# Two blocks of hedgehog linear attention and a ReGLU MLP on one core: the attention's inputs, its query side and the MLP's norm are computed in another way, and the plan is made anew

## The chip, the core and the metric

The kernel runs on one core of one Trainium2 chip. The metric is the device time of one execution in microseconds (us). The core's engines are named as in the profile: PE is TensorE's matmul, PEld its weight load, DVE is VectorE, ACT is ScalarE, POOL is GpSimd, and SP is SyncE, whose queue (SPq) issues nearly all DMAs here.

## What is computed

The input `x` has 2048 tokens of 512 bf16 values. Two layers follow each other, each an attention A and an MLP B, both on a layer-normed input and both added to `x`. The same weights serve both layers.

```python
def _A_ref(x, wqkv, w_phi, wo):          # 32 heads of 16
    q, k, v = split(x @ wqkv)
    pq, pk = q @ w_phi, k @ w_phi        # per head, 16x16
    phi_q = concat(softmax(pq), softmax(-pq))
    phi_k = concat(softmax(pk), softmax(-pk))
    kv, z = phi_k^T v, sum_s phi_k       # over all 2048 tokens
    num, den = phi_q kv, phi_q z + 1e-6
    return (num / den) @ wo

def _B_ref(x, W_gate, W_up, W_down):     # 512 -> 1376 -> 512
    return (relu(x @ W_gate) * (x @ W_up)) @ W_down

x = x + _A_ref(_layernorm(x)); x = x + _B_ref(_layernorm(x))   # twice
```

The sums `kv` and `z` run over all tokens. So no query can be answered, and no MLP of that layer can begin, before the keys of all 16 token tiles are summed.

## The kernel before

**Tiles.** The tokens lie in 16 tiles of 128 (`t`), in four chunks of four (`c`). `x` stays in SBUF as `X` and is updated in place. `w_phi` is folded into the key and query weights once, at the start (`fold`, L755 on: turns of the weight by PE, L767, or by DMA, L762, and products with a block-diagonal `Wblk`, L775).

**Attention, keys** (class `Keys`). Each tile is normed on DVE (batch-norm statistics L810 and L811, scale and centre L825; the root on ACT, L818 and L820), and turned to feature-major `xnTA` by PE or by DMA (`turn`, L784 on). PE multiplies it with the folded key weight (L849) and with the value weight (L855). ACT takes Exp of plus and minus the keys (`ek`, L852). DVE sums over each head (L860), ACT makes the reciprocal by Ln and Exp (L867, L870), and DVE or POOL multiply it in, half a tile at a time (`phi`, L879). PE adds the tile to the sums in PSUM with eight 65-column products (L896). After the 16th tile DVE builds the operand `R` (eight pairs, L918 and L924).

**Attention, queries.** The query projection is feature-major: one product gives 128 features for a chunk of 512 tokens (L937), and ACT takes both Exps (L941). In `attend`, PE multiplies a token tile's 128 columns of `Eq` with `R` (eight products of 144 columns, L955): 16 values, the sum of the Exps, and the normalizer for each head. ACT or DVE carry them out of PSUM in six copies (L752, L753). DVE forms the two weights (L971 to L977), multiplies (L980) and adds plus and minus (L985). The result is turned (L787, or L797 on PE), multiplied with `wo` (L992), and added to `X` (L997 for the first two tiles, which also takes the row sum; L1001 for the others).

**MLP** (`mlp`). It goes over groups of 1, 2 or 4 tiles (`BLOCKS`). Each tile gets batch-norm statistics again (L810, L811), is centred (L1018 or L1022) and turned. PE computes gate and up, feature-major, with 128 columns for each tile of the group (L1068), and the last 96 features token-major (L1044). ACT takes the Relu (L1072), ACT or DVE copy `up` out (L752, L753), DVE multiplies (L1076), PE multiplies with `W_down` (L1101), and DVE scales by the reciprocal of the variance and adds to `X` (L1108). For the first layer, the keys of a tile for the second layer begin as soon as its `X` is done.

**What sets the order.** Every operation is recorded as an `Op` with an engine, a cost, a due number and its dependences. `plan` (L82) then walks an event-driven list: it takes the operation that can go first, and the numbers in `DUE` break ties. Its result is the order in which each engine's instructions stand; the chip's engines run them in that order and wait for semaphores. The string `PLACE` chooses the engine of each operation that has two (evacuations and `phi`). PSUM has two banks for the sums and for L955 (`q`), and six for all else (`b`). Until the first L896, gaps that the plan sees on PE are filled with products of zeros (`idle`, L746), so that the clock stays up.

## Time and profile before

| what | value |
|---|---|
| median of 3 runs | 383.91 us (383.69 to 384.04) |
| the profiled execution | span 382.0 us from its first to its last instruction |
| what lies around the span, by the median | 1.9 us |
| granted TensorE clock | 1.00 |
| busy: PE, DVE, ACT, POOL | 371.5, 311.1, 215.0, 41.9 us |
| first L955 (all keys of layer 0 are summed) | 54.4 us |
| first L1068 (first gate product) | 63.86 us |
| first L955 and first L1068 of layer 1 | 237.47 us, 247.38 us |
| the last group of matmuls ends | 378.58 us |

The profile's slices are 9.55 us each. A matmul's duration in the profile is from its start to its result (379 ns for 512 columns), and successive ones overlap: L849 takes 0.86 us for four, so 216 ns each. For PE the spacing counts, not the duration. DVE's and ACT's durations overlap a little too: eight Exps of L941 stand in 4.30 us, 538 ns each, where the duration of one is 629 ns.

### The profile page before, as it was taken

The numbers are of one execution on the slowest core, as the hardware profiler recorded it, in microseconds if no ns is written. First come the engines' busy times: TensorE is split into PE (matmuls) and PEld (weight loads), VectorE is DVE, ScalarE is ACT, GpSimd is POOL, SyncE is SP. The second block draws the span as 40 slices with busy tenths as digits, with TensorE's granted clock in tenths as the row PEclk, the third lists the DMA queues.
The fourth block names the chain that finished last, engine by engine and source line by source line (L and its number), as shares of the span: only waits on it lengthen the run. The fifth ranks groups of instructions, "written<-read, shape, count | busy, mean of one in ns | idle before, by whom it ended". The sixth has DMA issues, their size and how long they took to land.

```text
span 382.0 us, 7622 instructions
## 1 busy us (share of the span) xinstructions
PE 371.5 (97%) x2787; PEld 224.4 (59%) x2832; DVE 311.1 (81%) x798; ACT 215.0 (56%) x554; POOL 41.9 (11%) x44
## 2 busy tenths in 40 slices
PE   7999998999989999999999999999999999999996
PEld 4545456967545445554656654696855544467575
DVE  7999999999999989983694677999998976763334
ACT  6999989636445316772455679984526412243040
POOL 0276710000200000230020124000000000000000
PEclk9999999999999999999999999999999999999999
DMA  8497720222221321211200100013322221020110
GB/s 232 122 205 219 188 89 2 52 58 62 57 56 41 44 54 40 45 23 27 45 6 15 22 8 1 2 36 70 77 44 70 57 56 56 14 62 16 41 50 29
DMA packets 60869, 22.83 MB, mean 60 GB/s; under 512 B 52672, under 2 KB 59808, under 8 KB 60832
## 3 DMA queue, kind: packets, MB, share of 16 engines
q1 hardware_dynamic: 60416, 21.95, 24.9%
q8 instruction: 22, 0.36, 0.4%
q10 hardware_dynamic: 416, 0.39, 0.4%
q14 instruction: 15, 0.12, 0.1%
HBM read 7.91 MB, written 2.10 MB: 26 GB/s over the span
## 4 chain that ended last, share of the span: by engine, by line
PE 77%; DVE 17%; DMA 2%; issue 2%; ACT 1%; DVEq 0%
PE b L1068 31%; PE b L1101 17%; PE b L855 5%; PE b L849 5%; PE b L992 5%; PE b L937 5%; PE q L955 3%; PE b L1044 2%; PE q L896 2%; DMA xnTA<-xn 2%; DVE pr L980 1%; DVE bstA L810 1%; DVE bstB L810 1%; DVE sk L860 1%; DVE N L753 1%
## 5 line engine op out<-in xcount | busy, mean ns | idle before, releaser
L1068 PE MATMUL b<-xnTB,wgu 128*128 128x128 bf16 (+2 forms) x1191 | 152.3, 279 | 0.5
L1068 PEld LDWEIGHTS <-wgu 128*128 128x128 bf16 x1200 | 97.7, 98 | 42.5
L1072 ACT ACTIVATE gu<-b 128x512 bf16<-128x512 f32 (+1 forms) x83 | 48.0, 584 | 63.7 <-PE b L1068 61.3
L1101 PE MATMUL b<-wd,hT 128*128 128x512 bf16 (+3 forms) x349 | 82.3, 372 | 0.7
L879 POOL TENSOR_TENSOR phiK<-ek,sk 128x512 bf16<-128x512 bf16 x38 | 41.2, 1102 | 192.3 <-ACT sk L870 164.1
L1101 PEld LDWEIGHTS <-hT 128*128 128x128 bf16 (+1 forms) x363 | 34.7, 98 | 33.9 <-DVE hT L1076 0.2
L1076 DVE TENSOR_TENSOR hT<-gu 128x512 bf16<-128x512 bf16 (+1 forms) x83 | 34.0, 414 | 15.4 <-ACT gu L752 14.2
L1108 DVE SCALAR_TENSOR_TENSOR X<-b,rsB,X 128x512 bf16<-128x512 f32 (+1 forms) x33 | 23.7, 729 | 23.8 <-PE b L1101 23.8
L752 ACT CAST gu<-b 128x512 bf16<-128x512 f32 (+1 forms) x50 | 28.4, 570 | 24.0 <-PE b L1068 20.4
L860 DVE TENSOR_REDUCE sk<-ek 128x64 f32<-128x1024 bf16 x32 | 38.6, 1210 | 2.7 <-ACT ek L852 2.3
L852 ACT ACTIVATE ek<-b 128x512 bf16<-128x512 f32 x64 | 36.0, 616 | 8.3 <-PE b L849 8.1
L941 ACT ACTIVATE Eq<-b 128x512 bf16<-128x512 f32 x64 | 37.3, 629 | 3.3 <-PE b L937 3.1
L752 ACT CAST N<-q 128x384 bf16<-128x384 f32 (+1 forms) x59 | 26.1, 464 | 12.4 <-PE q L955 6.7
L855 PE MATMUL b<-wv,xnTA 128*128 128x512 bf16 x123 | 31.9, 379 | 0.3
L937 PE MATMUL b<-xnTA,Wq 128*128 128x512 bf16 x125 | 31.9, 379 | 0.2
L849 PE MATMUL b<-Wk,xnTA 128*128 128x512 bf16 x123 | 31.6, 379 | 0.4 <-DVE xnTA L753 0.2
L992 PE MATMUL b<-wo,oT 128*128 128x512 bf16 x120 | 31.3, 379 | 0.4
L753 DVE CAST gu<-b 128x512 bf16<-128x512 f32 (+1 forms) x33 | 21.8, 665 | 11.1 <-PE b L1068 11.1
L955 PE MATMUL q<-R,Eq 128*128 128x144 bf16 x256 | 27.5, 226 | 1.8 <-DVE N L753 1.3
L955 PEld LDWEIGHTS <-Eq 128*128 128x128 bf16 x256 | 20.3, 98 | 13.1 <-issue 2.6
L980 DVE TENSOR_TENSOR pr<-N,w 128x1024 bf16<-128x1024 bf16 x32 | 21.8, 683 | 0.7
L810 DVE BATCH_NORM_STATS2 bstA<-X 128x6 f32<-128x512 bf16 x32 | 21.3, 682 | 1.2 <-DMA X<-in_A_x_dram 1.0
(75 smaller groups left out, 388.9 us busy)
## 6 DMA issues: line engine op xcount, KB each, us to landing
out_dram<-X SPq DMA_DIRECT2D x15, 128.0 KB, 1.7
X<-in_A_x_dram SPq DMA_DIRECT2D x6, 256.0 KB, 3.3
wgu<-in_B_W_gate_dram SPq DMA_DIRECT2D x4, 344.0 KB, 3.4
wgu<-in_B_W_up_dram SPq DMA_DIRECT2D x4, 344.0 KB, 3.5
wd<-in_B_W_down_dram SPq DMA_DIRECT2D x5, 256.0 KB, 3.5
wv<-in_A_wqkv_dram SPq DMA_DIRECT2D x2, 256.0 KB, 4.7
wo<-in_A_wo_dram SPq DMA_DIRECT2D x4, 128.0 KB, 3.1
oT<-o SPq DMA_TRANSPOSE x28, 2.3
```

The source lines that it names most:

```text
L752: both = {"ACT": ("ACT", act(cols), lambda: nc.scalar.copy(out=out_(), in_=in_()), False), "DVE": ("DVE", dve(cols), lambda: nc.vector.ten ...
L849: k = op("PE", mm(4, 512), due, lambda: [nc.tensor.matmul(kp.t[:], lhsT=xnTA[c][:, b, cols], rhs=Wk2[:, b, :], start=(b == 0), stop=(b == ...
L855: v = op("PE", mm(4, 512), due_v, lambda: [nc.tensor.matmul(vp.t[:], lhsT=xnTA[c][:, b, cols], rhs=wv[:, b, :], start=(b == 0), stop=(b == ...
L860: a = op("DVE", SUM16, due, lambda: nc.vector.tensor_reduce(out=sk.t[:, row, :], in_=ek.t[:].rearrange("p g s (h f) -> p (g s h) f", f=DH) ...
L879: e.tensor_tensor(out=ph.t[:].rearrange("p g s (h f) -> p (g s h) f", f=DH)[:, lo:lo + n], in0=ek.t[:].rearrange("p g s (h f) -> p (g s h) ...
L937: q = op("PE", mm(4, 512), due(c, b), lambda b=b, qp=qp: [nc.tensor.matmul(qp.t[:], lhsT=Wq2[:, m, b * P:(b + 1) * P], rhs=xnTA[c][:, m, : ...
L941: done.append(op("ACT", act(512), due(c, b), lambda b=b, s=s, qp=qp: nc.scalar.activation(out=Eq[c][:, b, s, :], in_=qp.t[:], func=AF.Exp, ...
L955: pe.append(op("PE", mm(len(groups), GE), due, lambda ps=ps, groups=groups: [nc.tensor.matmul(ps.t[:, n * GE:(n + 1) * GE], lhsT=Eq[c][:, ...
L992: a = op("PE", mm(4, 512), due + 3, lambda: [nc.tensor.matmul(yp.t[:], lhsT=oT.t[:, b, :], rhs=wo[:, b, :], start=(b == 0), stop=(b == NB ...
L1068: nc.tensor.matmul(ps.t[:, q * W:(q + 1) * W], lhsT=wgu[:, s, b, g * P:(g + 1) * P], rhs=xT.t[:, b, 0:W], start=(b == 0), stop=(b == NB - 1))
L1072: nc.scalar.activation(out=gu.t[:, 0, 0:cols], in_=gp.t[:, 0:cols], func=AF.Relu)
L1101: nc.tensor.matmul(yp.t[:, 0:c1 - c0], lhsT=h.t[:m, f * W + i * P:f * W + (i + 1) * P], rhs=wd[:m, f, c0:c1], start=(f == 0), stop=(f == N ...
```

## The change

1. **No normed copy of `x` for the attention.** Keys, queries and values are projected from raw `x`. Its turned copy `xT` comes by DMA straight from the input (layer 0, nine transposes) or from `X` (layer 1). The mean is taken out of the folded weights: `fold` computes each weight row's mean (32 one-column products, a copy, and a bias on the evacuations). The root scales the Exps (`scale=rs` and `-rs`, POOL makes the negative) and the evacuation of the values. What the mean contributes to the values is carried as a 66th column of the sums and taken off when `R` is built. The query weight is now loaded and turned by PE; it was turned by DMA.
2. **Token-major queries.** One query projection gives one token tile. Its Exps are summed on DVE, inverted on ACT, multiplied in place on POOL or DVE, as for the keys, and the 128x1024 result is turned by one DMA (`fq`). So each product with `R` is 68 columns wide and gives the finished numerator and denominator; the denominators are inverted (ACT, or DVE's reciprocal), and one multiply from PSUM writes `o`.
3. **MLP norm from sums.** The residual add takes the row sum for every tile; the sum of squares comes from ACT (`Square`) or DVE. The batch-norm statistics of the MLP go.
4. **`up` without a copy.** Where `PLACE` says DVE (33 of 83), DVE multiplies directly from PSUM; before, it copied and then multiplied.
5. **`phi` in place**, one pool of 22 buffers for keys and queries, seven `fq` buffers, and one PSUM buffer of two banks where two of one bank were.
6. **The plan** has other constants (landings of DMAs, costs, a delay of transposes in flight when PE fetches instructions), new `DUE` and `PLACE`, and each query projection must follow a certain key projection (`QKEY`).

The core of the diff:

```diff
-GV = GQ + 1
-GE = HB * (DH + 2)
+GV = GQ + 2
+GE = HG * (DH + 1)
...
-XPOSE, XPOSE_LOADS = (1245, 3600), (1245, 3600)
+XPOSE, XPOSE_LOADS = (1255, 2440), (1280, 3010)
...
-PHI0 = ["POOL", "POOL", "DVE"] * 5 + ["BOTH"]
-SUM_ON_PE, SPLIT, SUMMED = False, False, 2
+SUM_ON_PE, SPLIT = False, False
+QKEY = ((10, 11, 12, 13, 14, 15), (12, 13, 14, 15))
...
-    p_q, p_b = psum("q", 2), psum("b", 6)
+    p_q, p_b = psum("q", 1, [NG, P]), psum("b", 6, [512])
...
+        mp = Buf(p_b)
+        a = op("PE", (16 * 32, 16 * 32 + 170, 16), due, lambda: [nc.tensor.matmul(
+            mp.t[:, b:b + 1], lhsT=w[:, m, b * P:(b + 1) * P], rhs=less[:, 0:1], start=(m == 0), stop=(m == NB - 1))
+            for b in range(NB) for m in range(NB)], loaded + [c_less], [mp], name="means")
...
             e = [op("ACT", act(512), due, lambda s=s: nc.scalar.activation(
-                out=ek.t[:, :, s, :], in_=kp.t[:].rearrange("p (g e) -> p g e", e=GQ), func=AF.Exp, scale=1.0 - 2.0 * s), ...
+                out=ek.t[:, :, s, :], in_=kp.t[:].rearrange("p (g e) -> p g e", e=GQ), func=AF.Exp,
+                scale=(minus if s else plus)[:, t:t + 1]), [k, root[s]], ...
...
+    def query(l, t, due, ready, behind, key):
+        q = op("PE", mm(4, 512), due, lambda: [nc.tensor.matmul(
+            qp.t[:], lhsT=xT[c][:, b, cols], rhs=Wq2[:, b, :], ...) for b in range(NB)], ...)
+        e = [op("ACT", act(512), ..., func=AF.Exp, scale=(minus if s else plus)[:, t:t + 1]) for s in range(2)]
+        a = op("DVE", SUM16, ..., name="sq", follow=behind)
+        a = op("ACT", RLN[0], ..., name="lnq")
+        a = op("ACT", REXP[0], ..., name="rq")
+        a = halves("phq", ek, lambda: ek.t[:], lambda lo, n: sq.t[:, lo:lo + n], PHI["POOL"], ...)
+        a = op("SP", XWIDE, due, lambda: nc.sync.dma_start_transpose(
+            out=fq.t[:], in_=ek.t[:].rearrange("p g s e -> p (g s e)")), a, [fq], [ek], name="fq", move=1450)
...
+        pe = [op("PE", SUMS, due, lambda: [nc.tensor.matmul(
+            ps.t[:, g, 0:GE], lhsT=fq.t[:, g, :], rhs=R[:, g, :], start=True, stop=True) for g in range(NG)], ...
+        a = op("DVE", dve(512), due, lambda: nc.vector.tensor_tensor(out=o..., in0=ps.t[:, :, 0:GQ]..., in1=rd..., op=Alu.mult)
...
-            a = stats(l, "B", t, due_x(i), [after[t]])
+            seen.append(op("ACT", SQUARE, due_x(i), lambda t=t: nc.scalar.activation(
+                out=wasteA[:], in_=x_of(t), func=AF.Square, accum_out=ssq[:, l, t:t + 1]), [after[t]], name="ssq", ...
...
+            def direct(up=up, gu=gu, cols=cols, f0=f0):
+                nc.vector.tensor_tensor(out=h.t[:, f0 * W:f0 * W + cols], in0=gu.t[:, 0, 0:cols], in1=up.t[:, 0:cols],
+                                        op=Alu.mult)
```

How many instructions stand on each engine, as the two programs are built (DMA issues under SP):

| | before | after |
|---|---|---|
| PE, matmuls | 2832 | 2867 |
| of them the products with `R` | 256 of 144 columns | 256 of 68 columns |
| DVE | 794 | 531 |
| ACT | 555 | 564 |
| POOL half-tile multiplies (`phi`) | 38 | 86 |
| DVE half-tile multiplies (`phi`) | 26 | 42 |
| SP, all; transposes of 128x512 or smaller; of 128x1024 | 149; 101; 0 | 175; 87; 32 and 7 of 256 tokens |

## The prediction

> **What bounds the kernel now.** First the page's head, then the busy time by stretches. I cut at the first product with `R` (L955), the first gate product (L1068) and the first gate product of layer 1.
>
> ```profile
> span 382.0 us, 7622 instructions
> PE 371.5 (97%) x2787; PEld 224.4 (59%) x2832; DVE 311.1 (81%) x798; ACT 215.0 (56%) x554; POOL 41.9 (11%) x44
> ...
> PE 77%; DVE 17%; DMA 2%; issue 2%; ACT 1%; DVEq 0%
> ```
>
> ```profile
> 0.00:54.40 54.40, 51.76 (x378) 26.67 (x386) 50.34 (x105) 48.40 (x132) 23.91 (x28) 1.00 0.72 185
> 54.40:63.86 9.46, 8.03 (x66) 4.82 (x67) 8.54 (x28) 9.29 (x29) 0.00 (x0) 1.00 0.00 0
> 63.86:247.38 183.52, 180.99 (x1317) 108.76 (x1337) 154.96 (x389) 105.78 (x271) 17.95 (x16) 1.00 0.17 34
> 247.38:382.00 134.62, 130.73 (x1032) 84.20 (x1044) 97.30 (x278) 51.49 (x126) 0.00 (x0) 1.00 0.20 48
> ```
>
> The columns are PE, PEld, DVE, ACT, POOL, clock, DMA share, GB/s. From 63.86 us on PE hardly waits: it is the bound. In the first 54.4 us PE, DVE and ACT are all nearly full, so there no engine's gain counts alone.
>
> A matmul's duration overlaps its neighbours', so I take PE's cost from spacing in the timeline:
>
> ```profile
> 50.19 0.67 PE L896 MATMUL q<-vext,phiK 128*128 128x65 bf16 x16
> 50.70 1.02 PE L937 MATMUL b<-xnTA,Wq 128*128 128x512 bf16 x4
> ...
> 65.65 0.48 PE L955 MATMUL q<-R,Eq 128*128 128x144 bf16 x5
> 65.96 0.49 PE L1044 MATMUL b<-wgu,xnTB 128*128 128x192 bf16 x4
> ```
>
> Sixteen 65-column products take 0.51 us to the next start: 32 ns each. Five of 144 columns take 0.31: 62 ns. In the same way 128 columns cost 56 ns, 192 cost 82, 256 cost 109 and 512 cost 216. With the counts in the program, PE's work is 369.4 us. I call **lag** an instruction's start less the work ahead of it. It is 54.4 - 49.3 = 5.1 us at the first L955, 63.9 - 56.5 = 7.4 at the first gate product, 247.4 - 238.1 = 9.3 at that of layer 1, and 378.6 - 369.4 = 9.2 at the end. After the last matmul come 3.4 us (add, store). So span = PE work + lag + 3.4 = 382.0, and the median lies 1.9 us above that span.
>
> **The change, part by part.**
>
> *PE work.* The 256 products with `R` shrink from 144 to 68 columns: at 32 ns, 256 x (62 - 32) = -7.8 us. The means of two weights add 32 one-column products: +1.0. The column sums of the value weight add four of 512 columns, and one filler goes: +0.6. Turns balance (16 of a weight come, 24 of `xn` go, 8 of `X` come). Sum -6.1: 363.3 us. All the rest is lag.
>
> The Trainium skill ("TensorE: Matmul & The Clock Gate", "Back-to-back issue gap") says that in a real stream the spacing also carries the weight load, about 81 ns at 128 columns. The trace disagrees (56 ns; 32 at 65 columns). By the rule narrow products would gain little; that is rival D.
>
> *The front.* Nothing may pass `R`, so the sums ahead of it count, taken in the order of each engine with mean durations. DVE: 55.8 us in 97 instructions before; after, 55.8 in 88. Gone are 16 centrings (L825, 6.4), three half multiplies (2.1) and the fill of `R`; six query sums come (6 x 1.21 = 7.3, the row of L860), and 1.4 for the value sums. ACT up to the last key's reciprocal: 59.5 before, 58.9 after. PE ahead of the first product with `R`: 49.3 before, 53.6 after, because all 16 query projections now stand ahead of it; before, 2.6 us of them stood behind.
>
> So the norm that was removed is replaced, on DVE, by work of the same size. Three things come on top:
> - The first key Exp (10.75 us before) waits for the folded weight, and the fold now needs the means (16 x 32 ns), a copy of 0.17, and all four turned blocks (four evacuations of 0.6 on two engines) where each of its products needed one. I take +1.6; the bounds are 0 (input landing alone decides) and +3.
> - From the first head sum (12.49 us) to `R` (52.52) DVE ran 40.0 us for 43.8 us of durations. After, 46.7 stand there: 42.7 us at that ratio.
> - POOL does 29 half multiplies up to the last key's, where it did 22 in the first stretch. The rows of L879 show what a collision with DVE is:
>
> ```profile
> L879 POOL TENSOR_TENSOR phiK<-ek,sk x38: 1055/1057/1561, 15.7 to 233.2; 128x512 bf16<-128x512 bf16 x38
> ...
> L879 DVE TENSOR_TENSOR phiK<-ek,sk x26: 658/680/1269, 20.5 to 233.2; 128x512 bf16<-128x512 bf16 x26
> ```
>
> The longest are 0.5 to 0.6 us above the median. Eight such DVE multiplies stand ahead of `R`; each may wait between 0 and a POOL multiply (1.06): 0 to 8.5 us. I take two collisions, 1.0, as most of the 26 before ran undisturbed, though POOL was busy for only 23.9 of 54.4 us.
>
> The Trainium skill ("SBUF — State Buffer", "SBUF: two separate sides") calls the port of DVE and GpSimd an exclusive lock: the later of the two blocks for the whole instruction, where DVE reads two SBUF inputs. The trace's tails agree; rival B is what that would cost at worst.
>
> `R` begins at 12.49 + 1.6 + 42.7 + 1.0 = 57.8 us. Its build took 1.9 (52.52 to 54.40); the four new instructions (0.3 + 0.7 + 0.7 + 0.2) take as much. First product: **59.7 us**, work 53.6, lag 6.1.
>
> *From `R` to the first gate product.* Before: 9.46 us, with query projections as filler. After: products 0.45; Ln and Exp of the denominators about 0.55 with gaps (small ACT instructions, 0.22); the multiply 0.7; then turn, `wo`, add, centre and turn as before, 4.97 (58.89 to 63.86 in the timeline); 0.3 for Exps queued ahead on ACT. Sum 7.0 where PE has 3.4 of work, so lag grows by 3.6, against 2.3 before. First gate product: **66.7 us**, lag 9.7.
>
> *The rest.* Between the two `R`s DVE's durations fall from 182 to 158 us, behind the second from 132 to 99 (norm statistics, six copies and four small steps of each tile, direct `up`). That is worth nothing: PE is the bound there. It pays only for cover. ACT falls from 128 to 121 and 81 to 78. Query work that now comes later: ten head sums (12 us on DVE) and 28 half multiplies of layer 0, 21 of them on POOL (22 us), stand behind the last key's. Beside them PE has two one-tile MLPs of 7.2 us (80 x 56 + 4 x 82 + 11 x 216 ns) and the next groups. Two queries are ready to turn before `R`; POOL finishes the next two 3 and 5 us after the last key, and with a landing of 2.3 to 4.6 us they come about when PE reaches them. The 32 wide transposes are not in the trace: issue between one and two narrow ones (1.2 to 2.4 us on SPq), landing between 2.3 (row `oT<-o`) and twice that. SPq waited for data most of the time, and later queries are made many us before use: I take nothing, and up to +3 for late ones. The single PSUM buffer makes the next tile's products wait for this one's multiply, 1.8 us a tile against 8 us of PE work: nothing. At the layer change ACT ran 16.30 of 17 us before (228 to 245); after, 20.8 us of durations stand between the last tile's root and the first turned output, 16.7 with the overlap seen on Exps (538 ns against 629). PE has 18 us of work there. I take +0.5, bounds -0.5 and +3. Lag after the first gate product: 1.8 as before, +0.5.
>
> *Sum.* 363.3 + 9.7 + 1.8 + 0.5 + 3.4 = 378.7 us span; with 1.9, **380.6 us**, 0.9% less than 383.91.
>
> **The rivals.**
> - A, full gain: the start and the lock cost nothing, and lag at the first gate product stays 7.4. 363.3 + 7.4 + 1.8 + 3.4 + 1.9 = 377.8. For: ACT's sum ahead of `R` is smaller, and `x` arrives turned. Against: DVE's equal sum starts later.
> - B, slower: DVE and POOL block each other ahead of `R`. At 0.9 us for each of eight multiplies in place of 1.0 in all, +6.2: 386.8. It decides against the change once the first gate product comes after 70.0 us (lag 13.0, which eats the 6.1). For: POOL nearly without pause. Against: medians 680 and 1057 sit close to the minima.
> - C, late queries: after the first groups PE waits for head sums, multiplies and wide transposes, in all 3 us: 383.6. For: DVE was 97% busy from 60 to 160 us (9.6 to 9.9 of each 10), a small slip spreads. Against: DVE is relieved by 24 us there.
> - D, the narrow products don't get shorter: +7.8, 388.4. Against: the row of L896 above.
>
> **How the numbers follow.** Chances: forecast (378 to 383) 0.58, A 0.17, B 0.13, C 0.10, D 0.02. About 0.2% (383.1 to 384.7) can't be told from no change. Faster is the forecast, A, and a little of C: 0.76; the same 0.09; slower B, D and the rest of C: 0.15. The range, 376.3 to 386.5, takes in A with a little less start lag, C, and the lower part of B.
>
> **What would show it.** Right: the 68-column products spaced at 32 ns; the first at about 59.7 us; the first gate product at about 66.7; PE's lag then growing by some 2 us to the end; DVE with idle time in the MLP stretches. Wrong: a first gate product before 64 (A) or after 70 (B, with long POOL or DVE multiplies before it); PE waiting for `fq` or `oT` behind 70 us (C).

## The result, and the profile after

The changed kernel takes 397.49 us (median of 4 runs, 396.94 to 398.14) where the kernel before takes 383.83 us (4 runs beside it, 383.69 to 384.04): a ratio of 1.0355, with a 95% interval of 1.034 to 1.0369. The change makes the kernel 13.7 us slower. The forecast was 380.6 us, faster, with a range up to 386.5: its sign was wrong, and the time lies outside the range.

The page of the changed kernel, first its head and its chain (time on the path that ended last, by engine):

```profile
span 396.0 us, 7641 instructions
...
PE 370.6 (94%) x2820; PEld 218.7 (55%) x2867; DVE 283.0 (71%) x578; ACT 230.0 (58%) x580; POOL 108.0 (27%) x150
...
PE 53%; ACT 18%; DVE 17%; issue 4%; DMA 4%; POOL 1%; SPq 1%; DVEq 0%; ACTq 0%; POOLq 0%
```

PE's share of the chain fell from 77% to 53%, and ACT's rose from 1% to 18%. An engine that is busy for 58% of the span lies on that chain for some 70 us: the average hides a stage. The stretches, cut at the same three products as before (the first with `R`, the first gate product, the first gate product of layer 1), say which one. Columns: PE, PEld, DVE, ACT, POOL, granted clock, DMA share, GB/s.

```profile
0.00:64.96 64.96, 57.05 (x424) 29.28 (x433) 53.31 (x93) 57.77 (x146) 40.97 (x65) 1.00 0.73 171
64.96:73.71 8.75, 5.13 (x51) 3.26 (x52) 6.79 (x11) 6.47 (x20) 7.96 (x8) 0.80 0.49 92
73.71:261.30 187.59, 180.13 (x1325) 105.55 (x1344) 144.09 (x286) 111.46 (x286) 49.15 (x70) 0.99 0.32 56
261.30:396.00 134.70, 128.32 (x1031) 80.66 (x1043) 78.79 (x191) 54.34 (x130) 9.96 (x10) 0.99 0.35 69
```

The first stretch grew from 54.4 to 65.0 us. ACT's busy time in it grew from 48.4 to 57.8, DVE's only from 50.3 to 53.3. In every 10 us between 10 and 60 us ACT is busy for 9.94 to 10.00; in the kernel before it had been 9.45 to 10.00, between 10 and 50 us. Behind it two further things show: in the second stretch PE works for 5.1 of 8.75 us, at a granted clock of 0.80, and in the third it waits longer than it did before.

In ACT's queue just ahead of `R` the cause can be read. The first column is the start, the second the duration, both in us:

```profile
51.57 0.75 ACT L690 ACTIVATE ek<-b,rsA 128x512 bf16<-128x512 f32 x1
52.14 0.76 ACT L690 ACTIVATE ek<-b,nrs 128x512 bf16<-128x512 f32 x1
52.71 0.77 ACT L764 ACTIVATE ek<-b,rsA 128x512 bf16<-128x512 f32 x1
53.28 0.78 ACT L764 ACTIVATE ek<-b,nrs 128x512 bf16<-128x512 f32 x1
...
64.43 2.05 ACT L764 ACTIVATE ek<-b,nrs 128x512 bf16<-128x512 f32 x3
66.14 0.43 ACT L787 ACTIVATE rd<-q 128x32 f32<-128x32 f32 x1
```

Exps that stand back to back start 570 ns apart. Their inputs are named `b,rsA` and `b,nrs`: besides PSUM they read their scale from a tile in SBUF, the root of the layernorm (L690, L764), which is what the change folded into them. In the kernel before the input is `b` alone, and the starts are 478 ns apart. The last two lines show what that does behind `R`: its first product was issued at 64.96 us, but the Ln of its denominators (L787) began only at 66.14, behind three such Exps of later queries. PE waited for 2.2 us at its next step for it:

```profile
PE b L616 <- DVE o L793: 2.2, 1, 2.2
PE q L783 <- DVE R L745: 1.0, 1, 1.0
PE b L799 <- ACT oT L550: 0.7, 1, 0.7
```

I use the prediction's own measure, the lag (start of an instruction less PE's work ahead of it, by the same spacings), for the kernel before, the forecast, the changed kernel, and three of the experiments below. All in us:

| | before | forecast | changed | e1_const | e13_both_less | e15_all_less |
|---|---|---|---|---|---|---|
| PE work | 369.4 | 363.3 | 363.3 | 363.3 | 363.3 | 363.3 |
| lag, first product with `R` | 5.1 | 6.1 | 11.4 | 4.9 | 4.3 | 3.9 |
| lag, first gate product | 7.4 | 9.7 | 16.7 | 8.9 | 7.4 | 7.2 |
| lag at 110 us of work | 8.6 | | 20.7 | 12.5 | 11.8 | 11.1 |
| lag at 230 us of work | 9.1 | | 21.6 | 13.0 | 12.3 | 11.6 |
| lag at the end of PE | 9.2 | 12.0 | 28.1 | 17.5 | 16.0 | 14.7 |
| behind PE | 3.4 | 3.4 | 4.6 | 4.6 | 3.4 | 3.4 |
| span | 382.0 | 378.7 | 396.0 | 385.4 | 382.7 | 381.4 |

The span missed by 17.3 us: 5.3 ahead of `R`, 1.7 from there to the first gate product, 9.1 behind it, 1.2 behind PE. Two parts of that aren't the change's. The time behind PE lies between 3.4 and 4.6 us in runs that end with the same instructions; the median landing of the two last stores (64 KB) is 2.2 us in the changed kernel and in e1_const, 1.6 in the kernel before and in e13_both_less. And the first key Exp came at 13.67 us in this execution, against 12.14 to 12.58 in three runs below that also keep the changed kernel's Exps (e3_half_turn, e5_late_queries, e9_half_sums_after): more than 1 us of the 5.3 is a late start.

### The profile page after: what moved, and what is told of

The parts are those of the page before. It is cut to its first block, busy times and chain, and to the rows that moved or that the text cites. A ratio compares the mean times of both kernels' runs of the same rounds, so it can differ in the third digit from the quotient of the medians.

```text
span 396.0 us, 7641 instructions
## 1 busy us (share of the span) xinstructions
PE 370.6 (94%) x2820; PEld 218.7 (55%) x2867; DVE 283.0 (71%) x578; ACT 230.0 (58%) x580; POOL 108.0 (27%) x150
## 2 busy tenths in 40 slices
DMA packets 94965, 31.75 MB, mean 80 GB/s; under 512 B 86256, under 2 KB 93904, under 8 KB 94928
## 4 chain that ended last, share of the span: by engine, by line
PE 53%; ACT 18%; DVE 17%; issue 4%; DMA 4%; POOL 1%; SPq 1%; DVEq 0%; ACTq 0%; POOLq 0%
PE b L873 28%; PE b L913 13%; ACT ek L764 6%; ACT ek L690 5%; PE b L799 4%; DVE sq L767 3%; DVE ek L659 2%; DVE sk L703 2%; PE b L849 2%; PE b L687 2%; DVE o L793 2%; PE b L694 2%; DVE X L803 2%; ACT vext L547 2%; DMA oT<-o 2%
## 5 line engine op out<-in xcount | busy, mean ns | idle before, releaser
L913 PE MATMUL b<-wd,hT 128*128 128x512 bf16 (+2 forms) x354 | 83.3, 372 | 0.4
L659 POOL TENSOR_TENSOR ek<-ek,sq 128x512 bf16<-128x512 bf16 x43 | 47.2, 1117 | 52.3 <-ACT sq L772 42.9
L659 POOL TENSOR_TENSOR ek<-ek,sk 128x512 bf16<-128x512 bf16 x43 | 45.6, 1077 | 28.6 <-ACT sk L715 24.2
L703 DVE TENSOR_REDUCE sk<-ek 128x64 f32<-128x1024 bf16 x32 | 38.5, 1212 | 11.6 <-ACT ek L690 11.1
L767 DVE TENSOR_REDUCE sq<-ek 128x64 f32<-128x1024 bf16 x32 | 38.3, 1210 | 3.8 <-ACT ek L764 2.0
L892 ACT CAST gu<-b 128x512 bf16<-128x512 f32 (+1 forms) x50 | 28.1, 562 | 19.3 <-PE b L873 18.8
L890 DVE TENSOR_TENSOR hT<-gu,b 128x512 bf16<-128x512 bf16 (+1 forms) x33 | 22.2, 676 | 15.4 <-PE b L873 15.3
L761 PE MATMUL b<-Wq,xT 128*128 128x512 bf16 x124 | 30.5, 379 | 2.3 <-ACT ek L764 2.0
L687 PE MATMUL b<-Wk,xT 128*128 128x512 bf16 x120 | 31.4, 379 | 1.3 <-ACT ek L690 0.6
L694 PE MATMUL b<-wv,xT 128*128 128x512 bf16 x121 | 31.3, 379 | 1.0 <-DMA xT<-X 0.6
L690 ACT ACTIVATE ek<-b,rsA 128x512 bf16<-128x512 f32 x32 | 22.3, 700 | 3.1 <-PE b L687 3.0
L793 DVE TENSOR_TENSOR o<-q,rd 128x512 bf16<-128x512 f32 x32 | 21.9, 684 | 2.7 <-ACT rd L790 2.6
L764 ACT ACTIVATE ek<-b,rsA 128x512 bf16<-128x512 f32 x32 | 23.5, 766 | 0.0
```

Of the source, the lines that this page charges most:

```text
L659: e.tensor_tensor(out=out().rearrange("p g s (h f) -> p (g s h) f", f=DH)[:, lo:lo + n], in0=ek.t[:].rearrange("p g s (h f) -> p (g s h) f ...
L687: k = op("PE", mm(4, 512), due, lambda: [nc.tensor.matmul(kp.t[:], lhsT=xT[c][:, b, cols], rhs=Wk2[:, b, :], start=(b == 0), stop=(b == NB ...
L690: e = [op("ACT", act(512), due, lambda s=s: nc.scalar.activation(out=ek.t[:, :, s, :], in_=kp.t[:].rearrange("p (g e) -> p g e", e=GQ), fu ...
L694: v = op("PE", mm(4, 512), due_v, lambda: [nc.tensor.matmul(vp.t[:], lhsT=xT[c][:, b, cols], rhs=wv[:, b, :], start=(b == 0), stop=(b == N ...
L703: a = op("DVE", SUM16, due, lambda: nc.vector.tensor_reduce(out=sk.t[:, row, :], in_=ek.t[:].rearrange("p g s (h f) -> p (g s h) f", f=DH) ...
L761: q = op("PE", mm(4, 512), due, lambda: [nc.tensor.matmul(qp.t[:], lhsT=xT[c][:, b, cols], rhs=Wq2[:, b, :], start=(b == 0), stop=(b == NB ...
```

## The experiments

The theories: **O**, the operand: an ACT instruction that reads its scale or bias from SBUF takes 92 ns longer, 149 times, some 75 of them ahead of the first denominators. **T**: the wide transposes of the query features are late or crowd the DMA queue. **P**: the order was made for the wrong prices. **Q**: the three queries that moved ahead of `R` are missing behind it. The kernel before, beside which each group ran, took 383.99 to 384.34 us.

| run | us | ratio to before, 95% interval |
|---|---|---|
| e1_const | 387.22 | 1.0085, 1.006 to 1.011 |
| e2_before_operand | 388.63 | 1.0117, 1.01 to 1.0134 |
| e3_half_turn | 397.91 | 1.0348, 1.031 to 1.0385 |
| e4b_plan_price | 416.22 | 1.0837, 1.0821 to 1.0853 |
| e5_late_queries | 396.49 | 1.0318, 1.0296 to 1.034 |
| e6_late_const | 388.70 | 1.0120, 1.0104 to 1.0136 |
| e7_price_late | 422.61 | 1.1002, 1.0952 to 1.1052 |
| e8_half_sums | 386.25 | 1.0050, 1.0033 to 1.0067 |
| e9_half_sums_after | 397.05 | 1.0332, 1.0315 to 1.035 |
| e10_new_order | 399.61 | 1.0415, 1.0364 to 1.0466 |
| e11_no_inverse | 387.84 | 1.0079, 1.0061 to 1.0097 |
| e12_turn_early | 385.99 | 1.0045, 1.0025 to 1.0065 |
| e13_both_less | 384.96 | 1.0020, 1.0011 to 1.0029 |
| e14_pool_less | 384.46 | 1.0007, 0.9998 to 1.0017 |
| e15_all_less | 383.64 | 0.9986, 0.9972 to 1.0001 |
| e16_both_late | 386.44 | 1.0063, 1.0047 to 1.0078 |

### The operand, taken away and put in

e1_const gives the Exps of the changed kernel the constant scales of the kernel before, and copies the values unscaled:

```diff
-                scale=(minus if s else plus)[:, t:t + 1]), [k, root[s]], [ek] if s == 0 else [],
+                scale=1.0 - 2.0 * s), [k, root[s]], [ek] if s == 0 else [],
...
-                     [v, root[0]] + ones, [vx], [vp], "vext", times=lambda: plus[:, t:t + 1])
+                     [v, root[0]] + ones, [vx], [vp], "vext")
...
-            scale=(minus if s else plus)[:, t:t + 1]), [q, root[s]], (), [qp, ek], name="Eq") for s in range(2)]
+            scale=1.0 - 2.0 * s), [q, root[s]], (), [qp, ek], name="Eq") for s in range(2)]
```

> Leaves out the root: the Exps of keys and queries take the constant scales 1 and -1 and the values are copied out unscaled; every engine's instructions stand in the same order as in the changed kernel. Theory O (an ACT instruction that reads its scale from SBUF costs about 92 ns more, spacing 570 instead of 478 ns; 62 Exps and 8 value copies stand ahead of the first denominators): the spacing of the Exps goes back to 478 ns, the first product with R comes 5 to 6 us earlier (near 59.5 us), the first gate product near 67, the layer change loses 2 to 3 us less, and the time falls by 8 to 10 us to about 388. Theory T (wide transposes and DMA crowding make the kernel late): the Exps get faster but the time falls by less than 3 us. Theory C (the longer chain from R to the first gate product and the idle PE's clock): the first product moves earlier, but lag still grows by over 5 us from there to the first gate product.

e2_before_operand goes the other way: in the kernel before, the Exps read the same +1 and -1 from two columns of a tile.

```diff
+    sc = new("sc", [2], F32)
...
-                out=ek.t[:, :, s, :], in_=kp.t[:].rearrange("p (g e) -> p g e", e=GQ), func=AF.Exp, scale=1.0 - 2.0 * s), [k], [ek] if s == 0 else [],
+                out=ek.t[:, :, s, :], in_=kp.t[:].rearrange("p (g e) -> p g e", e=GQ), func=AF.Exp, scale=sc[:, s:s + 1]), [k], [ek] if s == 0 else [],
```

(and the same for `Eq`).

> The kernel before, with one thing added: the 128 Exps read their scale (1 or -1) from a two-column SBUF tile instead of an immediate. The result and the order are unchanged. Theory O: spacing 570 instead of 478 ns, so 128 x 92 ns = 11.8 us more on ACT, of which the 58 Exps ahead of the first products with R (ACT full there) cost about 5 us and those at the layer change 1 to 3: time 388 to 392. Theories T and C, in which the operand is no matter: 384, unchanged.

Measured: 387.22 us, 10.3 less than the changed kernel, and 388.63 us, 4.6 more than the kernel before. The rows of the query's Exp, of the kernel before, of e2_before_operand and of e1_const (shortest, median and longest duration in ns, then first and last start):

```profile
L941 ACT ACTIVATE Eq<-b x64: 578/614/753, 18.9 to 248.4; 128x512 bf16<-128x512 f32 x64
```

```profile
L943 ACT ACTIVATE Eq<-b,sc x64: 667/742/1039, 19.8 to 253.2; 128x512 bf16<-128x512 f32 x64
```

```profile
L764 ACT ACTIVATE ek<-b x64: 577/676/880, 31.5 to 246.5; 128x512 bf16<-128x512 f32 x64
```

The shortest is the one with the least overlap: 578 and 577 ns with a constant, 667 with the operand, whatever the kernel. Of e1_const's stretches the first is the one to read:

```profile
0.00:58.45 58.45, 55.47 (x424) 28.98 (x433) 52.65 (x93) 52.33 (x148) 40.26 (x65) 1.00 0.77 191
58.45:65.94 7.49, 5.29 (x52) 3.18 (x53) 6.51 (x11) 5.14 (x18) 7.49 (x8) 0.77 0.73 89
```

With the same order of instructions, the first product with `R` comes at 58.45 instead of 64.96 us: its lag falls by 6.5, where 5 to 6 had been expected. Of these 1.4 lie ahead of the first key Exp (13.67 against 12.22 us) and are the late start of the changed kernel's profiled execution. From that Exp to `R` it is 51.3 us in the changed kernel, 51.2 in e3_half_turn and in e9_half_sums_after, and 46.2 in e1_const: 5 us for the operand. (The edit also takes 63 ns off each of DVE's 16 value copies, of which 5 stand ahead of `R`: 0.3 us.) From `R` to the end the lag gives back another 4.1. Theory O holds, in both directions. It accounts for 10.3 of the 13.7 us, and leaves 3.2 us against the kernel before, although PE has 6.1 us less to do: some 9 us are still to be found.

### The wide transposes

e3_half_turn turns only half of each query's features and reads each turned group twice, so a transpose moves 128x512 instead of 128x1024.

```diff
-            out=fq.t[:], in_=ek.t[:].rearrange("p g s e -> p (g s e)")), a, [fq], [ek], name="fq", move=1450)
+            out=fq.t[:, 0:NB, :], in_=ek.t[:, 0:NB].rearrange("p g s e -> p (g s e)")), a, [fq], [ek], name="fq", move=1450)
...
-            ps.t[:, g, 0:GE], lhsT=fq.t[:, g, :], rhs=R[:, g, :], start=True, stop=True) for g in range(NG)],
+            ps.t[:, g, 0:GE], lhsT=fq.t[:, g % NB, :], rhs=R[:, g, :], start=True, stop=True) for g in range(NG)],
```

> Leaves out half of the query features: each of the 32 wide transposes turns 128x512 instead of 128x1024, and the products with R read each turned group twice. All other instructions as in the changed kernel. Theory T: issue on the SP queue halves (the first four took 10.95 us), narrow transposes behind them land earlier, and the time falls by 3 to 6 us. Theory O: less than 1 us, as ACT's queue sets the front and the layer change.

Measured: 397.91 us, no change, though the DMA queues moved 27.55 instead of 31.75 MB. The width of these transposes isn't what costs while ACT holds up `R`: theory T falls in this form. Whether they are late is asked again in e12_turn_early, without the operand.

### The order and its prices

The planner's list has one price for an ACT instruction of 512 columns (`act(512)`), with or without an operand. e4b_plan_price adds 95 ns where there is one:

```diff
+OPERAND = 95
...
-            e = [op("ACT", act(512), due, lambda s=s: nc.scalar.activation(
+            e = [op("ACT", act(512, more=OPERAND), due, lambda s=s: nc.scalar.activation(
```

(and the same for the queries' Exps and for copies with a scale or a bias).

> The changed kernel, whose planner is told that an Exp or a copy with its scale or bias in SBUF takes 95 ns more, so that the order of the instructions is the one that it finds best at that price; the same work. If the 10 us that the constant scales gave back are the instructions' own durations (theory O), a better order can return little: 395 to 398 us. If they come from an order made for the wrong price (buffers taken by the wrong instruction, queues that turn up late), most of them return without any change of the instructions: 388 to 391 us.

Measured: 416.22 us, a miss of both expectations, and far slower. PE's longest wait between 55 and 90 us (us in all, times, longest):

```profile
PE q L730 <- POOL ek L662: 6.1, 1, 6.1
```

PE now waits 6.1 us for a key's multiply on POOL. The due times belong to one set of prices; at another the same due times give an order in which the last keys come late. A truer price in the list is worth nothing without new due times. With 92 in place of 95 ns the same due times give no complete order at all: the list comes to a point at which no instruction can go (e4_plan_price, for which there is therefore no time). e7_price_late has the same prices, and three queries held back as in the next section:

> The planner told the price of 95 ns and the last three queries of the first layer held back; the same work as the changed kernel. If theories O and Q hold and add to each other: 389 to 393 us, still slower than the kernel before, because 149 instructions keep their 92 ns. If the order is not worth anything: 396 to 398 us.

Measured: 422.61 us, missed in the same way. For e10_new_order due times and places were searched anew in the planner's own model, at 92 ns for an operand and 230 ns for POOL's small operations (the list has 150; the trace's medians are 210 and 230).

```diff
-        b = op("POOL", (150, 200), dues[-1], lambda: nc.gpsimd.tensor_scalar(
+        b = op("POOL", (230, 280), dues[-1], lambda: nc.gpsimd.tensor_scalar(
...
-DUE = (
-    316, 222, 319, 170, 199, 169, 168, 203, 421, 278, 232, 207, 265, 213, 14, 296, 20, 19, 236, 17, 0, 13, 15, 205,
...
```

> The changed kernel's own instructions, with due times and places of the movable copies searched anew at prices nearer to the traces' (92 ns more for an Exp or a copy with its scale or bias in SBUF, 230 ns for POOL's small operations). e4b_plan_price (416.2 us) had the price without new due times. If part of the 14 us is an order made for the wrong prices (theory P), a fitting order returns a third to a half of it: 389 to 393 us. If it is the instructions' time alone, which no order hides, ACT stays the bound ahead of R: 396 to 398 us. If it came to under 384 us, the change would have been worth it with a right plan.

Measured: 399.61 us, above both expectations. The first product with `R` did come earlier (61.9 us), but behind it PE waits again. Its longest wait between 55 and 100 us:

```profile
PE q L788 <- DMA fq<-ek: 2.3, 1, 2.3
```

So the order that the change brought is no worse than any of these three, and theory P isn't supported. That a longer search, or one on the chip, would find a better one isn't excluded.

### Queries held back

In the kernel before, three of the first layer's 16 query projections stood behind the first product with `R`; in the changed one none does. e5_late_queries puts three behind again (e6_late_const does it on top of e1_const):

```diff
+        asked[l, t] = q
...
+        for t, n in (((13, 0), (14, 1), (15, 2)), ())[l]:
+            asked[l, t].follow.append(asks[l][n])
```

> The changed kernel with the last three queries of the first layer held back: their products on PE may start only behind the first, second and third product with R, as in the kernel before, where three queries stood there. Theory Q: the queries ahead of R are a second cause beside the operands; six Exps of 570 ns and three pairs of Ln and Exp of some 330 ns, 4.4 us of ACT's queue, leave the path to R, and 2.6 us of PE's work move from ahead of it into the wait behind it. The first product with R then comes at some 61 us instead of 65.0, and the time falls to 391 to 394 us. Rival: the chain of products, denominators, transposes and sums behind R sets the first gate product, and the held back Exps stand in its way on ACT as they did before: 396 to 398 us.

> Both together: constant scales and unscaled value copies (leaves out the root, as e1_const does) and the last three queries of the first layer held back. Theory Q says that what e1_const (387.2 us) still loses against the kernel before sits in the gap behind R, in which PE has nothing to do but wait, and in the lower clock that follows it; with 2.6 us of products to fill it: 383.5 to 385 us, and a granted clock of 1.0 between 60 and 70 us. If the rest sits elsewhere (the waits of the MLP stretch, the layer change): 386.5 to 388 us.

Measured: 396.49 and 388.70 us. The first moved `R` from 65.0 to 63.0 us and gained 1 us, not 4; the second gained nothing on e1_const, and lies above both of its ranges. In e6_late_const PE waits 3.3 us for the first product with `R`, which comes at 58.48 us, just where it came in e1_const (58.45). Theory Q falls in this form: PE's work was moved out of the way of something that wasn't waiting for PE.

### What is left when the scales are constant

These runs all start from e1_const and take work away from one engine after another, in the same order of instructions. e8_half_sums (and e9_half_sums_after on the changed kernel itself) shortens DVE's query sums:

```diff
-            out=sq.t[:], in_=ek.t[:].rearrange("p g s (h f) -> p (g s h) f", f=DH), axis=AX.X, op=Alu.add),
+            out=sq.t[:], in_=ek.t[:].rearrange("p g s (h f) -> p (g s h) f", f=DH)[:, :, 0:DH // 2], axis=AX.X, op=Alu.add),
```

> e1_const (387.2 us; constant scales, so the root is left out) in which the queries' sums on DVE add 8 of the 16 features of each group, 512 elements instead of 1024 (leaves out the other half of these sums); the same order of instructions. Theory D: with the operands' price gone, DVE is what PE waits for behind the first gate product and at the layer change (DVE was busy 18.98 of 20 us there), so 32 sums that are 0.6 us shorter give back most of the 6 us by which the lag still grows behind the first gate product: 382 to 384 us. Rival: the chain's latencies (products, denominators, transposes) and POOL's multiplies set these waits, and DVE only looks full: 386 to 387.5 us.

> The changed kernel itself with the halved query sums (leaves out half of these sums). Ahead of R it is ACT that is full (theory O), so the first product with R stays at some 64 to 65 us; only the waits behind the gate product and at the layer change can shrink. Theory D with O: 393 to 396 us. If DVE were the bound ahead of R too: 388 to 391 us. If neither: 397 to 398 us.

e11_no_inverse drops the Ln (L770) and the Exp (L772) of the query sums from ACT's queue:

> e1_const (387.2 us, leaves out the root) without the Ln and the Exp that turn the queries' sums into their inverse on ACT (leaves out that inverse; the features are multiplied by the sums themselves); the same order. Theory A: with the operands' price gone, ACT is still what R waits for (busy 9.84 to 10.00 of every 10 us from 10 to 55), and these pairs, some 0.3 us each, 13 of them ahead of R, are the work that the token-major queries added there: the first product with R comes 3 to 4 us earlier, at 54.5 to 55.5 instead of 58.45 us, and the time is 383.5 to 385 us. Rival: DVE's and POOL's work ahead of R ends no earlier than ACT's, and the time stays at 386 to 387.5 us.

e12_turn_early lets the wide transposes read a tile that lies still:

```diff
-            out=fq.t[:], in_=ek.t[:].rearrange("p g s e -> p (g s e)")), a, [fq], [ek], name="fq", move=1450)
+            out=fq.t[:], in_=wv[:, 0:2, :].rearrange("p b f -> p (b f)")), a, [fq], [ek], name="fq", move=1450)
```

> e1_const in which the 32 wide transposes turn columns of the value weights, which lie still in SBUF, instead of the queries' features, and the denominators' Ln and Exp are other functions of the same shape so that the numbers stay finite (leaves out the query side of the result): sums, inverses, multiplies and transposes are all issued in the same order, but no product with R waits for the chain from a query's Exps over its sum, inverse and multiply to the landing of its transpose. Theory L: it is the length of this chain that PE waits for behind R and at the layer change (waits for the landing of features, 0.9 us between 228 and 295 us in e1_const, and for what the late products hold up): the growth of the lag behind the first gate product falls from 8.6 to 4 to 6 us, and the time to 382.5 to 385 us. Rival: the chain behind the products (denominators, output transposes, sums) sets these waits, and the time stays at 386.5 to 388 us.

Measured: 386.25, 397.05, 387.84 and 385.99 us. None comes out as its theory (D, A, L) said; e11_no_inverse and e12_turn_early miss their rivals' ranges as well, by 0.3 and 0.5 us. e9_half_sums_after lies 0.4 us below the changed kernel; the single reliefs of e1_const (387.22) lie within 1.2 us of it, and their intervals overlap with its own. In e11_no_inverse the first product with `R` stays at 58.5 us. Then two engines, three, and three with the chain:

> e1_const with both reliefs at once: halved query sums on DVE and no inverse of these sums on ACT (leaves out the root, half of the sums and their inverse). Alone they gave 386.25 and 387.84 us, and left the first product with R at 57.7 and 58.5 us. Theory E, the engines are full together: now it comes at 54 to 56.5 us and the time is 383 to 385 us. Rival F, the fixed chain behind R and its waits: the first product comes a little earlier, and the time stays at 385.5 to 387.5 us.

e14_pool_less shortens POOL's multiplies (`phi(nc.gpsimd, k * H, H // 2)` in place of `H`), e15_all_less adds the still tile:

> e13_both_less with POOL's multiplies over half of their columns (leaves out the other half of these multiplies). POOL was busy 10.00 of 10 us from 30 to 60 us in e11_no_inverse, against 5.7 to 7.4 in the kernel before. If POOL is the third full engine (theory E): the first product with R at 52 to 55 us, 381.5 to 384 us. Rival F: as e13_both_less within 0.7 us.

> e14_pool_less with the wide transposes turned from a still tile, so that no product with R waits for its query's chain either (leaves out the query side of the result). Theory E: 381 to 383 us, near the 380.6 us of the forecast, which had the PE saving and no growth of waits. Rival F: 384.5 to 386.5 us; then only the chain from a product with R over denominators, output, its transpose and the sums to the gate products is left as what PE waits for.

Measured: 384.96, 384.46 and 383.64 us. Relieved together, DVE and ACT are worth 2.3 us, where alone they gave 1.0 and -0.6. The time lies just inside theory E's range. But theory E put the gain down to the time ahead of `R`, and this isn't what the profiles show: `R`'s first product comes at 57.9 us, no earlier than with DVE's relief alone (57.7), where PE hardly waits for it. The difference lies behind: from `R` to the first gate product the lag grows by 5.3 us in e8_half_sums and in e11_no_inverse, and by 3.1 in e13_both_less. A part of that is PE's clock (third column from the right), first in e11_no_inverse, then in e13_both_less:

```profile
60.00:65.00 5.00, 3.16 (x32) 2.10 (x33) 4.41 (x8) 2.48 (x7) 5.00 (x6) 0.70 0.56 105
65.00:70.00 5.00, 5.00 (x50) 3.90 (x48) 4.07 (x9) 2.38 (x8) 2.55 (x3) 0.62 0.47 82
```

```profile
57.90:64.40 6.50, 4.12 (x53) 2.59 (x53) 5.03 (x11) 4.48 (x12) 6.50 (x7) 1.00 0.50 94
```

e8_half_sums has the drop too (0.50 from 62.5 to 67.5 us) in its profiled execution, while the mean clock of its other three is 0.999 to 1.000, at 385.47 to 386.55 us. So the clock isn't all of it, and how much of the 2.3 us the joint relief is worth stays open. POOL's relief adds 0.5 (rival F's range) and the chain's 0.8 (between both ranges), each with intervals that overlap. But even the kernel from which all of this is taken away doesn't beat the kernel before by more than can be told from nothing (0.9972 to 1.0001), although PE has 6.1 us less to do. Its stretches behind `R`:

```profile
57.50:64.20 6.70, 4.17 (x54) 2.60 (x53) 4.85 (x11) 4.67 (x13) 3.08 (x6) 1.00 0.01 2
64.20:247.60 183.40, 179.62 (x1346) 104.89 (x1343) 133.47 (x286) 100.04 (x252) 30.90 (x70) 1.00 0.32 57
```

Over these stretches no engine but PE is near full, and still PE waits. In parts of them DVE is: it is busy for 5.00 of 5 us from 90 to 95 and from 100 to 105 us. PE's longest waits between 50 and 70 us, and between 70 and 125:

```profile
PE b L616 <- DVE o L791: 1.5, 1, 1.5
PE b L616 <- DVE xn L815: 0.6, 1, 0.6
PE b L797 <- ACT oT L550: 0.4, 1, 0.4
```

```profile
PE b L797 <- DVE hT L879: 1.1, 1, 1.1
PE b L871 <- DMA xnTB<-xn: 0.6, 1, 0.6
```

The first three are links of one chain: product with `R`, denominators and output on DVE, the turn, the product with `wo`, the sum, the centring, the turn, the gate product. Of the other two one is the landing of a turn, the other an MLP's multiply in DVE's queue. That fits rival F, the chain's latencies, which were left over when the engines were relieved; no run shortens them, and for the second group DVE's queue, full in parts, is a rival that none of these runs rules out. The table of lags shows the size of what is left: behind the first gate product the lag grows by 7.5 us in e15_all_less (7.2 to 14.7), by 8.6 in e1_const, by 1.8 in the kernel before.

The last run asks once more for the three queries, now that ACT and DVE have room:

> e13_both_less (384.96 us; leaves out the root, half of the queries' sums and their inverse) with the last three queries of the first layer held back behind the first three products with R, as in e6_late_const. Theory Q, second form: once ACT and DVE have room, PE's 53.6 us of work ahead of R is the bound there; with 2.6 us less of it the first product with R comes at 55 to 56 us instead of 57.9, the held back products fill the waits behind it, and the time is 382 to 383.5 us. Rival: R comes no earlier, since the last keys' chain sets it, and the held back products only change places with the wait: 384.3 to 385.8 us.

Measured: 386.44 us, 1.5 more than without it and above both ranges. The chain of e16_both_late up to the first product with `R` (start, duration):

```profile
51.01 1.50 POOL ek L659
52.51 1.25 POOL vext L700 x2
...
53.81 0.67 PE q L727 x16
...
55.34 0.27 PE q L727 x8
55.63 0.19 DVE R L749
...
56.78 1.00 DVE R L745
57.82 0.41 PE q L782 x8
```

It starts on POOL, at the last keys' multiply and the small products of mean and root (L700) behind it, and ends with 2.1 us of DVE's build of `R`. PE waited 2.2 us for it. So the first product stands at 57.5 to 58.5 us in all kernels with constant scales. Where DVE is relieved and the queries are ahead of it, PE's own work holds it (a lag of 3.9 to 4.3, and at most 0.2 us of waiting for `R`); in e1_const, e11_no_inverse and e12_turn_early PE waits 0.6 to 1.1 us for DVE's `R`; in e16_both_late the last keys hold it.

## Why the prediction was wrong, step by step

- **PE work, -6.1 us:** right. With its spacings the lag stays flat where PE doesn't wait (in the changed kernel 21.2 us at 170 us of work, and 21.2 at 210). Eight products of 68 columns take 0.25 us to the next start, 31 ns each, not the 62 of 144 columns (rival D falls).
- **ACT's sum ahead of `R`, "59.5 before, 58.9 after":** this is the step that failed. It was "taken in the order of each engine with mean durations", and the Exps got the duration of the kernel before, whose scale is a constant. The changed ones read it from SBUF, which no 512-column ACT row of the trace of before shows; the step should have bounded it as an operation not seen. By the prediction's own way of counting, the 63 such instructions that start before the last key's reciprocal ends add 5.8 us, which makes 64.7 where DVE has 55.8 and PE 53.6; up to the first denominators there are some 75 of them, 6.9 us. Measured, the operand moves `R` by 5 us and the time by 10.3. The Trainium skill ("ScalarE: Activation LUTs", "What ACT_TABLE_LOAD costs") states that each such pointer operand adds about 93 ns to an ACTIVATE. The traces agree (570 against 478 ns between starts), and the prediction overlooked it. Worked out from that figure of the Trainium skill alone, as an estimate, 75 x 93 ns = 7.0 us would have made the forecast 387.6 us, a slower kernel.
- **First key Exp, +1.6 with bounds of 0 and +3:** right. In the changed kernel's profiled execution it came at 13.67 us, +2.9, but in twelve of the other runs at 12.0 to 12.6 (+1.3 to +1.9), with the operand or without. That execution was late already at the first evacuation of the fold, 8.34 us against 6.87 to 7.50.
- **First product with `R` at 59.7, first gate product at 66.7 us:** 64.96 and 73.71. In e1_const, where ACT has the price that was assumed, they came at 58.45 and 65.94. From the first head sum (13.34 us) to `R` (56.18) DVE ran there for 42.8 us, where the prediction had 42.7. So the rest of the working for the front (DVE's stretch, the build, the chain to the gate) was right to 1.3 us.
- **Collisions, rival B:** the first gate product after 70 us is the sign that B had named, but its mechanism isn't there. Of seven DVE multiplies ahead of `R` (the prediction counted eight) one took 1267 and one 933 ns, the others some 680: 0.8 us in all, where the forecast took 1.0. The multiplies have the medians of before:

```profile
L659 POOL TENSOR_TENSOR ek<-ek,sq x43: 1047/1057/1622, 46.0 to 297.6; 128x512 bf16<-128x512 bf16 x43
L659 DVE TENSOR_TENSOR ek<-ek,sk x21: 628/684/1267, 44.6 to 240.4; 128x512 bf16<-128x512 bf16 x21
```

- **"Lag after the first gate product: 1.8 as before, +0.5":** the second step that failed, mis-sized even with O taken away: 11.4 us in the changed kernel, 8.6 with constant scales, 7.5 with every engine relieved. The saving of 7.8 us on the products with `R` was counted in full. A reading that fits, and that no run of its own shows: part of those products had stood beside the chain's waits, where PE had nothing else to do; shortened, they leave the wait longer. Rival C had the right place (PE waiting for `fq` and `oT` behind 70 us) and gave it 3 us, of which its own cause, late queries, is a small part: e12_turn_early gave back 1.2, with intervals that overlap. (That DVE was busy for 9.6 to 9.9 of each 10 us, as rival C has it, is misread from 120 to 140 us, where it was 18.54 of 20.)
- **Layer change, +0.5 with bounds of -0.5 and +3:** out of bounds in the changed kernel. From layer 1's first product with `R` (250.5 us) to its first gate product (261.3 us) PE has 6.3 us of work, and the lag grows by 4.5; PE's clock was 0.72 there from 255 to 260 us. With constant scales (241.95 and 249.54 us) it grows by 1.3, inside the bounds, so the rest comes with the operand. In the kernel before it was 0.2. Some 2 and 3 us of lag more come behind that gate product, where the prediction had nothing.
- **DVE with idle time in the MLP stretches, worth nothing:** right as an average; DVE is busy for 144.1 of 187.6 us where it was 155.0 of 183.5, and halving its query sums changed little. But from 80 to 100 us it is busy for 20.00 of 20: here too the average hides a stage.

What stays open: the cause of the lag that grows behind the first gate product, 7.5 us with every engine relieved. The chain's latencies and DVE's queue where it is full are the candidates; the latencies themselves, and another order of the links, were not tried. No experiment points to a version that beats the kernel before: the nearest, e15_all_less, does only a part of the work.

## What to carry to other kernels

An operation that is folded into another engine's instruction isn't free because the count stays the same: look up the form of operand that it gets, multiply the difference by all the instructions that get it, and add it to that engine's sum in the stage where it is full (here 92 ns, 75 times, on an engine that was busy for 58% of the span). PE work that is saved beside a chain of waits may turn into waiting; take the saving only for stretches in which PE's lag stays flat. And before the difference of two profiles is put down to an edit, compare what the edit can't have moved: the start, the end, and PE's clock.

## What the runs showed of the chip that was not expected

The granted clock of PE fell after stretches in which PE worked little, without standing still for long. In the changed kernel, between 62.5 and 72.5 us (clock in the third column from the right):

```profile
62.50:65.00 2.50, 1.46 (x9) 0.58 (x8) 2.43 (x6) 2.50 (x5) 2.50 (x3) 1.00 0.46 84
65.00:67.50 2.50, 0.38 (x8) 0.25 (x7) 1.67 (x3) 2.50 (x9) 1.84 (x2) 1.00 0.56 105
67.50:70.00 2.50, 1.70 (x16) 1.01 (x17) 1.88 (x3) 2.13 (x9) 2.36 (x3) 0.88 0.56 105
70.00:72.50 2.50, 1.86 (x18) 1.37 (x17) 2.04 (x6) 1.16 (x3) 2.50 (x3) 0.50 0.23 45
```

PE's longest pause there was 2.24 us, up to 67.62; some 4 us after the pause began its clock was at one half, and eight products with `R` took 0.47 us to the next start (70.22 to 70.69) where they took 0.25 at 73.46. In e1_const the clock is 0.50 between 62.5 and 65 us, after a stretch (57.5 to 60) with 0.72 of 2.5 us busy. An estimate from these windows (half the busy time at 0.50, and the shares at 0.89 and 0.93) puts the loss at 1.4 us. In the profiled executions of e12_turn_early and e13_both_less the clock stays at 1.00, and the lag at the first gate product is lower by 1.4 and 1.5 us. Little work alone doesn't decide it: e12_turn_early has only 0.59 of 2.5 us busy in the same stretch, and the mean clock of one kernel differs between executions (e8_half_sums: 0.991 once, 0.999 to 1.000 three times). What else decides isn't shown.
